# A block of unused TensorE products and cross-engine sums added inside the third FFN chunk

## The chip, the cores and the metric

The kernel runs on one core of one Trainium2 chip. The time is that of one execution on the device, in microseconds (us); lower is better. The core has a matrix engine (TensorE, "PE" in the profile, with "PEld" for its weight loads), a vector engine (VectorE, "DVE"), a scalar engine (ScalarE, "ACT"), GpSimd ("POOL") and SyncE ("SP"), which here only issues DMAs. Each engine runs its own instruction stream in order; the streams meet through semaphores.

## The reference

It is one transformer block with adaptive layer norm: linear attention, then a SwiGLU feed-forward network (FFN). S = 2048 rows, D = 1024, F = 3584, everything in bf16.

```python
sa, ca, ga, sb, cb, gb = (silu(c) @ w_mod) in six parts of 1024
h = layernorm(x) * (1 + ca) + sa
x = x + ga * linear_attention(h, wqkv, wo)       # 32 heads
h = layernorm(x) * (1 + cb) + sb
x = x + gb * ((silu(h @ w_gate) * (h @ w_up)) @ w_down)
```

## The kernel before

The program is written as plain Python calls, `P.pe(...)`, `P.act(...)`, `P.dve(...)`, `P.pool(...)` and `P.dma(...)`. A small planner, `_Prog`, notes for each call which bytes of SBUF and which PSUM banks it touches, and adds a semaphore wait wherever a call must come behind one of another engine. The order of the calls is the order of each engine's stream; nothing is rescheduled. For SBUF the planner knows reads from writes (a write waits for the last write and the last reads of the same bytes). For PSUM it does not: a bank belongs to the engine that used it last, and another engine that touches it waits. All compute instructions are recorded by one helper, so in the profile they all carry its line, L176 (L177 in the changed kernel).

The attention half takes the first part of the span. The FFN then goes over the 2048 rows in four chunks (`ch` 0 to 3) of 512 rows. The third chunk is `ch == 2`. A chunk has two stages:

- *Gate and up.* 28 steps (`ft` 0 to 27), one for each 128 columns of F. A step is eight 128x128x512 products of `GUG` with `H2T` into a gate bank and eight of `GUU` with `H2T` into an up bank. Then ACT takes Silu of the gate bank into `SG`, and DVE multiplies that with the up bank into `AT`. Even steps use banks 2 (gate) and 3 (up), odd steps banks 0 and 1. So the products of step `ft` have to wait until ACT and DVE have read what step `ft - 2` left in the same banks.
- *Down.* Four tiles of 128 rows (`j`), each 56 products of `AT` with `WD` (`WD_A` holds the first 16 blocks of w_down, `WD_B` the other 12) into a pair of banks, 4 and 5 or 6 and 7 by turns. ACT copies a bank out to `ATT`, DVE scales it and adds it to the residual `XRES`, and SP writes it out.

Weights for gate and up are loaded by SP into four slots, each as soon as TensorE has left it. During steps 4 to 7 of a chunk DVE also normalises the rows of the next one into `XN2`; after step 27 a DMA transposes them into `H2T` and POOL applies scale and shift (`th2_mod`).

The calls of a step, as they stand in the loop:

```python
P.act("activation", out=SG[:, ft % 2, :], in_=PS[:, gbank, :], func=ACT.Silu)
P.dve("tensor_tensor", out=AT[:, ft, :], in0=SG[:, ft % 2, :], in1=PS[:, ubank, :], op=ALU.mult)
```

Of the kernel before, what the change touches and what calls it, by code (L numbers as in the profile page):

```python
# [4 lines left out]

FP32 = mybir.dt.float32
BF16 = mybir.dt.bfloat16
U8 = mybir.dt.uint8
ACT = mybir.ActivationFunctionType
ALU = mybir.AluOpType  # L10
# [252 lines left out]
def bass_adaLN_cond__linear_attn_block__swiglu_ffn__prompt_kernel(  # L263
# [22 lines left out]
    with ExitStack() as es:  # L286
# [6 lines left out]
        def T(name, off, shape, dt):  # L293
            n = 1
            for s_ in shape[1:]:
                n *= s_
            assert off % 32 == 0 and off + n * mybir.dt.size(dt) <= ARENA, (name, off, shape)
            return nc.alloc_sbuf_tensor_at(name, shape, dt, offset=base + off)

        KB = 1024  # L300
        XRES = T("xres", 0, [128, NST, D], BF16)
        PQT = T("pqt", 32 * KB, [128, NHG, S], BF16)
        WCA = T("wca", 32 * KB, [128, NDT, D], BF16)
        WSA = T("wsa", 48 * KB, [128, NDT, D], BF16)
        AT = T("at", 72 * KB, [128, NFT, 512], BF16)
        SM = 64 * KB
        IDENT = T("ident", SM + 0, [128, 128], BF16)
        MASK = T("mask", SM + 256, [128, 128], BF16)
# [4 lines left out]
        MODTMP = T("modtmp", SM + 1088, [128, 16], BF16)  # L313
        MODCOL = T("modcol", SM + 1120, [128, 4, NDT], FP32)
        STATS = T("stats", SM + 1248, [128, 2, 4, 2, 6], FP32)
        MV = T("mv", SM + 1632, [128, NST, 2], FP32)
        VE = T("ve", SM + 1760, [128, NST], FP32)
        RSTD = T("rstd", SM + 1824, [128, NST], FP32)
        NEGHALF = T("neghalf", SM + 1888, [128, 4], FP32)
        SUMX = T("sumx", SM + 1920, [128, NST], FP32)  # L320
# [41 lines left out]
        WD_A = T("wd_a", 32 * KB, [128, 16, D], BF16)  # L362
# [7 lines left out]
        ATT = T("att", 190 * KB, [128, 2, 512], BF16)  # L370
        SG = T("sg", 184 * KB, [128, 2, 512], BF16)
        JUNK = T("junk", 186 * KB, [128, D], BF16)

        WDG = T("wdg", 144 * KB, [128, NFT, 128], BF16)

# [3 lines left out]
        PS = nc.alloc_psum_tensor("ps", [128, 8, 512], FP32)  # L379
# [15 lines left out]
        P = _Prog()  # L395
# [315 lines left out]
        def macc(src, kt):  # L711
            if kt == 0:
                P.dve("tensor_scalar", out=ACC[:], in0=src[:, kt, :], scalar1=SILUF[:, kt:kt + 1], scalar2=None,
                      op0=ALU.mult)
            else:
                P.dve("scalar_tensor_tensor", out=ACC[:], in0=src[:, kt, :], scalar=SILUF[:, kt:kt + 1], in1=ACC[:],
                      op0=ALU.mult, op1=ALU.add)

        def macc_split():
            P.dve("tensor_copy", out=MHL[:, 0, :], in_=ACC[:])  # L720
            P.dve("tensor_tensor", out=MHL[:, 1, :], in0=ACC[:], in1=MHL[:, 0, :], op=ALU.subtract)
            xbar(MHLT[:], MHL[:].rearrange("p i d -> p (i d)"))

        def mod_red():
            P.dve("tensor_reduce", out=RED[:], in_=MHLT[:].rearrange("d (i m) p -> d m i p", i=2),
                  axis=mybir.AxisListType.XY, op=ALU.add)
# [337 lines left out]
        def ln2_sq(st):  # L1064
            P.act("activation", out=JUNK[:], in_=XRES[:, st, :], func=ACT.Square, accum_out=SUMSQ[:, st:st + 1])
            if st % 4 == 3:
                ln2_rstd(st // 4)

        def gu_load(q):
            slot = q % 4  # L1070
            p = q % 14
            g_out, g_in = GUG[slot][:], wgv[:, :, p * 256:(p + 1) * 256]
            u_out, u_in = GUU[slot][:], wuv[:, :, p * 256:(p + 1) * 256]

            def fn(e):
                return [e.dma_start(out=g_out, in_=g_in), e.dma_start(out=u_out, in_=u_in)]

            P.add("sp", fn, reads=[], writes=[g_out, u_out], lane="gu%d" % slot, ninc=2, tag="gu_load")

        for st in range(NST):  # L1080
# [3 lines left out]
            if st < 4:  # L1084
                P.wait_for("sp", [done])
                if st < 3:
                    ch = st + 1
# [23 lines left out]
        for ch in range(NCH):  # L1111
            nxt = ch + 1 if ch + 1 < NCH else None
            for ft in range(NFT):
                q = 14 * ch + ft // 2
                slot = q % 4
                ftl = ft % 2
                gbank, ubank = 2 - (ft % 2) * 2, 3 - (ft % 2) * 2
                for dt in range(NDT):
                    P.pe("matmul", out=PS[:, gbank, :], lhsT=GUG[slot][:, dt, ftl * 128:(ftl + 1) * 128],
                         rhs=H2T[:, dt, :], start=(dt == 0), stop=(dt == NDT - 1))  # L1120
                for dt in range(NDT):
                    P.pe("matmul", out=PS[:, ubank, :], lhsT=GUU[slot][:, dt, ftl * 128:(ftl + 1) * 128],
                         rhs=H2T[:, dt, :], start=(dt == 0), stop=(dt == NDT - 1))
                P.act("activation", out=SG[:, ft % 2, :], in_=PS[:, gbank, :], func=ACT.Silu)
                P.dve("tensor_tensor", out=AT[:, ft, :], in0=SG[:, ft % 2, :], in1=PS[:, ubank, :], op=ALU.mult)
                if ftl == 1 and q + 4 < 14 * NCH:
                    gu_load(q + 4)
                if ch == 0 and ft % 2 == 0 and ft < 14:
                    i = ft // 2
                    wt = WD_A[:, 4 * i:4 * i + 4, :] if i < 4 else WD_B[:, 4 * i - 16:4 * i - 12, :]  # L1130
                    P.dma("wd%d" % i, wt, wdv[:, 4 * i:4 * i + 4, :])
                if ch == 0 and ft < 8:
                    macc(STGX[1], ft)
                if ch == 0 and ft == 8:
                    macc_split()
                if ch == 0 and ft == 11:
                    mod_red()
                    mod_row_a()
                if ch == 0 and ft == 12:
                    mod_row_b(6, 1, GB_B)  # L1140
                if nxt is None and ft in (8, 12):
                    f0, f1 = (0, 16) if ft == 8 else (16, NFT)
                    wt = WD_A if ft == 8 else WD_B
                    P.dve("tensor_tensor", out=WDG[:, f0:f1, :], in0=wt[:, :, 896:1024],
                          in1=GB_B[:, 896:1024].unsqueeze(1).to_broadcast([128, f1 - f0, 128]), op=ALU.mult)
                if nxt is not None and 4 <= ft < 8:
                    ln2_xn(4 * nxt + (ft - 4))
            if nxt is not None:
                th2_dma()
                th2_mod()  # L1150
            for j in range(4):
                st = 4 * ch + j
                bb = 4 + 2 * (st % 2)
                last = st == NST - 1
                if not last:
                    for ft in range(NFT):
                        for nh in range(2):
                            P.pe("matmul", out=PS[:, bb + nh, :], lhsT=AT[:, ft, j * 128:(j + 1) * 128],
                                 rhs=WD(ft)[:, nh * 512:nh * 512 + 512], start=(ft == 0), stop=(ft == NFT - 1))
                for nh in range(2):  # L1160
                    i = nh
                    parts = [(0, 384, bb + 1), (384, 512, 4)] if last and nh == 1 else [(0, 512, bb + nh)]
                    for (c0, c1, pb) in parts:
                        if last:
                            for ft in range(NFT):
                                P.pe("matmul", out=PS[:, pb, c0:c1], lhsT=AT[:, ft, j * 128:(j + 1) * 128],
                                     rhs=WDG[:, ft, :] if c0 > 0 else WD(ft)[:, nh * 512 + c0:nh * 512 + c1],
                                     start=(ft == 0), stop=(ft == NFT - 1))
                        xs = XRES[:, st, nh * 512 + c0:nh * 512 + c1]
                        gbs = GB_B[:, nh * 512 + c0:nh * 512 + c1]  # L1170
                        if c0 > 0:
                            P.dve("tensor_tensor", out=xs, in0=PS[:, pb, c0:c1], in1=xs, op=ALU.add)
                        else:
                            P.act("activation", out=ATT[:, i, c0:c1], in_=PS[:, pb, c0:c1], func=ACT.Copy)
                            P.dve("tensor_tensor", out=UT[:, i, c0:c1], in0=ATT[:, i, c0:c1], in1=gbs, op=ALU.mult)
                            P.dve("tensor_tensor", out=xs, in0=xs, in1=UT[:, i, c0:c1], op=ALU.add)
                        out_ops.append(P.dma("out", ov[:, st, nh * 512 + c0:nh * 512 + c1], xs))
# [37 lines left out]
```

## Time and profile before

| | |
|---|---|
| Measured times | 828.17 and 828.62 us, median 828.39 |
| Span of the profiled execution, first to last instruction | 827.0 us |
| TensorE busy | 817.0 us, 99% of the span, 4244 products recorded |
| VectorE busy | 310.8 us, 38% |
| ScalarE busy | 197.3 us, 24% |
| GpSimd busy | 40.7 us, 5% |
| Gate and up stage of the third chunk | from about 534.6 to 630.9 us of the span |

The profile is of one execution, of which the page gives the span; the measured times also contain what lies around it, 1.2 to 1.6 us here. In the lines of groups the columns are: kernel line, engine, operation, output <- inputs by tile name, shapes, count | busy time in us and mean duration of one in ns | idle time of the engine just before them, and what ended most of it. In the lines of the timeline they are: start and duration in us, engine, line, operation, tiles, shapes, count; in brackets the idle time before and what ended it. Products are pipelined: the duration of one includes the time until its result has drained, so the rate is read from starts, not from durations. Tile names are in lower case, `ps` is any PSUM bank.

### The profile page before, as it was taken

The numbers are of one execution on the slowest core, as the hardware profiler recorded it, in microseconds if no ns is written. First come the engines' busy times: TensorE is split into PE (matmuls) and PEld (weight loads), VectorE is DVE, ScalarE is ACT, GpSimd is POOL, SyncE is SP. The second block draws the span as 40 slices with busy tenths as digits, with TensorE's granted clock in tenths as the row PEclk, the third lists the DMA queues.
The fourth block names the chain that finished last, engine by engine and source line by source line (L and its number), as shares of the span: only waits on it lengthen the run. The fifth ranks groups of instructions, "written<-read, shape, count | busy, mean of one in ns | idle before, by whom it ended". The sixth has DMA issues, their size and how long they took to land.

```text
span 827.0 us, 10428 instructions
## 1 busy us (share of the span) xinstructions
PE 817.0 (99%) x4244; PEld 376.1 (45%) x4323; DVE 310.8 (38%) x664; ACT 197.3 (24%) x336; POOL 40.7 (5%) x59
## 2 busy tenths in 40 slices
PE   8999999999999999999999999999999999999998
PEld 4544444444444444444444444444444444444444
DVE  5798988476945521111221112122111211221111
ACT  4658643123241111011111101111110111111011
POOL 1010000000130000030000003000000300000000
PEclk9999999999999999999999999999999999999999
DMA  9969665856697995700455570045557004553000
GB/s 317 283 151 225 156 169 144 185 166 200 164 256 234 289 256 153 175 27 23 133 149 152 154 177 29 20 128 153 152 153 185 26 19 124 153 153 87 0 26 26
DMA packets 199360, 119.32 MB, mean 144 GB/s; under 512 B 57992, under 2 KB 183056, under 8 KB 199312
## 3 DMA queue, kind: packets, MB, share of 16 engines
q1 hardware_dynamic: 199296, 118.65, 53.7%
q8 instruction: 34, 0.56, 0.3%
q14 instruction: 14, 0.11, 0.0%
q10 hardware_dynamic: 16, 0.00, 0.0%
HBM read 100.67 MB, written 4.33 MB: 127 GB/s over the span
## 4 chain that ended last, share of the span: by engine, by line
PE 95%; DMA 2%; DVE 1%; SPq 1%; issue 1%; ACT 0%; DVEq 0%; ACTq 0%
PE ps L176 95%; DMA wsa<-in_w_mod_dram 2%; DVE acc L176 1%; SPq L176 1%; DVE pkt L176 0%; DVE e L176 0%; DVE pqt L176 0%; ACT e L176 0%; DVE xres L176 0%; DVE ht L176 0%; DVEq L247 0%; ACTq L247 0%
## 5 line engine op out<-in xcount | busy, mean ns | idle before, releaser
L176 PE MATMUL ps<-h2t,gug 128*128 128x512 bf16 x878 | 210.1, 379 | 0.9
L176 PE MATMUL ps<-h2t,guu 128*128 128x512 bf16 x878 | 209.9, 379 | 0.9
L176 DVE TENSOR_TENSOR at<-sg,ps 128x512 bf16<-128x512 bf16 x112 | 77.0, 688 | 282.7 <-PE ps L176 270.5
L176 ACT ACTIVATE sg<-ps 128x512 bf16<-128x512 f32 x112 | 66.9, 597 | 309.7 <-PE ps L176 298.3
L176 PEld LDWEIGHTS ps<-h2t,guu 128*128 128x128 bf16 x896 | 87.7, 98 | 105.7
L176 PEld LDWEIGHTS ps<-h2t,gug 128*128 128x128 bf16 x896 | 87.6, 98 | 105.5
L176 PE MATMUL ps<-wd_a,at 128*128 128x512 bf16 (+1 forms) x502 | 111.9, 377 | 0.5
L176 PE MATMUL ps<-ht,wqk 128*128 128x512 bf16 x499 | 110.5, 379 | 1.0 <-issue 0.2
L176 PE MATMUL ps<-wd_b,at 128*128 128x512 bf16 (+1 forms) x377 | 84.7, 377 | 0.4
L176 PEld LDWEIGHTS ps<-wd_a,at 128*128 128x128 bf16 x512 | 50.1, 98 | 59.7
L176 DVE TENSOR_TENSOR ut<-att,gb_b 128x512 bf16<-128x512 bf16 (+1 forms) x32 | 13.9, 435 | 167.2 <-ACT att L176 167.2
L176 PEld LDWEIGHTS ps<-ht,wqk 128*128 128x128 bf16 x512 | 49.4, 98 | 59.0 <-DVE ht L176 0.7
L176 ACT ACTIVATE att<-ps 128x512 bf16<-128x512 f32 (+1 forms) x32 | 17.4, 591 | 182.1 <-PE ps L176 182.1
L176 PEld LDWEIGHTS ps<-wd_b,at 128*128 128x128 bf16 x384 | 37.5, 98 | 44.7
L176 PE MATMUL ps<-pk,xres 128*128 128x512 bf16 x250 | 55.4, 379 | 0.6 <-issue 0.5
L176 PE MATMUL ps<-mw,pqt 128*128 128x512 bf16 x249 | 55.5, 379 | 0.5 <-issue 0.2
L176 POOL TENSOR_SCALAR h2t<-h2t,modcol 128x512 bf16<-128x512 bf16 x32 | 26.3, 837 | 383.4 <-DMA h2t<-xn 383.4
L176 ACT ACTIVATE e<-ps 128x512 bf16<-128x512 f32 x56 | 33.2, 604 | 31.9 <-PE ps L176 20.2
L176 PEld LDWEIGHTS ps<-mw,pqt 128*128 128x128 bf16 x256 | 24.7, 98 | 30.2 <-issue 0.5
L176 PEld LDWEIGHTS ps<-pk,xres 128*128 128x128 bf16 x256 | 24.7, 98 | 29.9 <-issue 0.9
L176 ACT ACTIVATE junk<-xres 128x1024 bf16<-128x1024 bf16 x24 | 25.4, 1058 | 34.5 <-DVE xres L176 34.2
L176 DVE SCALAR_TENSOR_TENSOR xres<-ps,xres 128x512 bf16<-128x512 f32 x32 | 21.4, 688 | 11.8 <-PE ps L176 11.6
(107 smaller groups left out, 337.9 us busy)
## 6 DMA issues: line engine op xcount, KB each, us to landing
gug<-in_B_w_gate_dram SPq DMA_DIRECT2D x56, 512.0 KB, 4.0
guu<-in_B_w_up_dram SPq DMA_DIRECT2D x56, 512.0 KB, 5.3
xres<-in_A_x_dram SPq DMA_DIRECT2D x20, 256.0 KB, 4.4
rb<-recip_den SPq DMA_DIRECT2D x8, 512.0 KB, 11.5
stgx<-in_w_mod_dram SPq DMA_DIRECT2D x2, 2048.0 KB, 9.7
wd_a<-in_B_w_down_dram SPq DMA_DIRECT2D x4, 1024.0 KB, 7.4
out_dram<-xres SPq DMA_DIRECT2D x31, 128.0 KB, 1.7
xres<-in_A_x_dram SPq DMA_DIRECT2D x3, 1024.0 KB, 7.1
```

The costliest lines, as they stand in the source:

```text
L176: return getattr(e, method)(**kw)
```

## The change

A function `probe()` is defined and called once, in the third chunk, behind the calls of step 16. Its results are used by nothing else. It has five new tiles, in SBUF bytes that are free during the FFN: `W4`, `X4` and `S4` in float32r, and three `F4` in float32. It reads `WD_A` (bf16), and uses PSUM banks 5 and 6.

```diff
+        W4 = T("w4", 100 * KB, [128, 4, 128], FP32R)
+        X4 = T("x4", 102 * KB, [128, 512], FP32R)
+        S4 = T("s4", 192 * KB, [128, 512], FP32R)
+        F4 = [T("f4%d" % i, (194 + 2 * i) * KB, [128, 512], FP32) for i in range(3)]
+
+        def probe():
+            b0, b1 = WD_A[:, 0, 0:512], WD_A[:, 1, 0:512]
+            P.dve("tensor_copy", out=W4[:].rearrange("p a b -> p (a b)"), in_=b0)
+            P.dve("tensor_copy", out=X4[:], in_=b1)
+            for i in range(32):
+                P.pe("matmul", out=PS[:, 5, :], lhsT=W4[:, i % 4, :], rhs=X4[:], start=(i == 0), stop=(i == 31))
+            for i in range(8):
+                P.pe("matmul", out=PS[:, 6, :], lhsT=W4[:, i % 4, :], rhs=X4[:], start=(i == 0), stop=False)
+                P.pe("matmul", out=PS[:, 6, :], lhsT=WD_A[:, i, 0:128], rhs=b0, start=False, stop=(i == 7))
+            for i in range(4):
+                P.act("activation", out=F4[0][:], in_=PS[:, 5, :], func=ACT.Copy)
+                P.dve("tensor_tensor", out=F4[1][:], in0=PS[:, 6, :], in1=F4[0][:], op=ALU.add)
+                P.pool("tensor_tensor", out=F4[2][:], in0=F4[1][:], in1=F4[0][:], op=ALU.add)
+                P.dve("tensor_tensor", out=F4[1][:], in0=F4[1][:], in1=F4[0][:], op=ALU.add)
+            for i in range(4):
+                P.dve("tensor_tensor", out=S4[:], in0=b0, in1=b1, op=ALU.subtract)
+                P.pool("tensor_tensor", out=S4[:], in0=b0, in1=b1, op=ALU.subtract)
+                P.act("activation", out=S4[:], in_=b1, func=ACT.Copy)
+                P.pool("tensor_copy", out=S4[:], in_=b1)
+            for i in range(4):
+                P.dve("tensor_tensor", out=S4[:], in0=b0, in1=F4[1][:], op=ALU.add)
+                P.pool("tensor_tensor", out=F4[2][:], in0=b0, in1=F4[0][:], op=ALU.add)
...
+                if ch == 2 and ft == 16:
+                    probe()
```

By the diff that is 48 products (40 float32r, 8 bf16), 18 instructions on DVE (two casts and 16 sums or differences), 16 on POOL (12 sums or differences, 4 copies) and 8 copies on ACT.

## The prediction

> **What bounds the kernel now.** I read the chain of waits first: it says which engine sets the end. Then the page's groups of instructions for durations, and last the timeline where the new work goes in.
>
> ```profile
> PE 95%; DMA 2%; DVE 1%; SPq 1%; issue 1%; ACT 0%; DVEq 0%; ACTq 0%
> ...
> L176 PE MATMUL ps<-h2t,gug 128*128 128x512 bf16 x878 | 210.1, 379 | 0.9
> L176 PE MATMUL ps<-h2t,guu 128*128 128x512 bf16 x878 | 209.9, 379 | 0.9
> L176 DVE TENSOR_TENSOR at<-sg,ps 128x512 bf16<-128x512 bf16 x112 | 77.0, 688 | 282.7 <-PE ps L176 270.5
> L176 ACT ACTIVATE sg<-ps 128x512 bf16<-128x512 f32 x112 | 66.9, 597 | 309.7 <-PE ps L176 298.3
> ```
>
> TensorE is 95% of the chain and idles 0.9 us before all 878 gate products, while DVE and ACT idle some 300 us waiting for it. So whatever TensorE is given is paid in full, and whatever the others are given is free until TensorE has to wait for it. The timeline at step 16 of the third chunk:
>
> ```profile
> 591.44 1.89 PE L176 MATMUL ps<-h2t,guu 128*128 128x512 bf16 x8
> 591.72 0.60 ACT L176 ACTIVATE sg<-ps 128x512 bf16<-128x512 f32 x1 [2.86 <-PE ps L176]
> ...
> 593.16 1.89 PE L176 MATMUL ps<-h2t,gug 128*128 128x512 bf16 x7
> 593.36 0.69 DVE L176 TENSOR_TENSOR at<-sg,ps 128x512 bf16<-128x512 bf16 x1 [2.76 <-PE ps L176]
> ```
>
> Step 16's up products start at 591.44 and step 17's gate products at 593.16: eight take 1.72 us, 0.2158 us each (the 379 ns of a row include the drain). A whole step is 16 products, 3.453 us. DVE's multiply starts 0.20 us after the next group has begun: that is how long a finished bank takes to be seen.
>
> **The change part by part.** Nothing is removed or moved. The instructions are inserted on PE, ACT, DVE and POOL between step 16 and step 17; no DMA is added, and SP is not touched.
>
> *1. The start.* The first float32r product waits for two DVE casts, which stand behind step 16's multiply on DVE. That multiply ends at 593.36 + 0.69 = 594.05. A cast of 512 elements between bf16 and f32 is a row: rcb<-rcp, 427 ns. Two give 594.91, a hop DVE to PE is 0.05 (mrow ends 289.05, the weight load begins 289.10). TensorE, free at 593.16, starts at 594.96: **1.8 us**, hidden by nothing.
>
> *2. The products.* 8 bf16 products at 0.2158 are 1.73. No row shows a float32r product. [...] Above: the weight load (98 ns in bf16) with twice the bytes and no longer beside the previous product, 0.2158 + 2 x 0.098 = 0.41. I take 0.2158, the row of the same shape: 40 x 0.2158 = 8.63. **10.4 us** together; the upper end adds 7.8.
>
> [...]
>
> *3. The chain behind the products.* The sums and copies share few buffers, so each waits for another engine. From bank 6's end, in the order of the waits in the compiled streams:
> - first loop, four turns: ACT copies bank 5 into f4[0], DVE adds bank 6, POOL adds the two, DVE adds again (it overwrites what POOL reads), and the next ACT copy overwrites f4[0], so it waits for both. The first ACT copy lies beside the last 16 products.
> - second loop, four turns: DVE, POOL, ACT, POOL, all writing s4, strictly one after the other.
> - third: four DVE sums behind the last POOL copy, with four POOL sums beside them.
>
> Prices: DVE sum with f32 0.69 (at<-sg,ps 688; den<-ps 683); ACT copy 0.60 (att<-ps 595). Hops: into POOL 0.12 (0.08 to 0.16 after DVE's ve), others 0.05. POOL has no 512-wide sum of two tensors. Nearest is its one-input row:
>
> ```profile
> L176 POOL TENSOR_SCALAR h2t<-h2t,modcol 128x512 bf16<-128x512 bf16 x32 | 26.3, 837 | 383.4 <-DMA h2t<-xn 383.4
> ```
>
> So a POOL sum lies between 0.84 and twice that, 1.67, if the inputs are read in turn; I take 1.2, nearer the one-input row. A POOL copy lies between 0.55 (a 256-wide memset at 0.311, scaled) and 0.84; I take 0.7. DVE's last four sums run beside POOL, which costs; see three lines of chunk 2's end, where POOL is busy from 641.16 to 647.91, and one later line without POOL:
>
> ```profile
> 644.48 0.88 DVE L176 TENSOR_TENSOR xres<-xres,ut 128x512 bf16<-128x512 bf16 x1
> 645.27 0.41 DVE L176 TENSOR_TENSOR ut<-att,gb_b 128x512 bf16<-128x512 bf16 x1
> 645.72 0.80 DVE L176 TENSOR_TENSOR xres<-xres,ut 128x512 bf16<-128x512 bf16 x1
> ...
> 656.48 0.42 DVE L176 TENSOR_TENSOR xres<-xres,ut 128x512 bf16<-128x512 bf16 x1
> ```
>
> Beside POOL the sum takes up to 0.4 more; I take 0.9 each (0.69 to 1.1).
>
> Loop one: 0.69 + 0.12 + 1.2 + 0.05 + 0.69 = 2.75, then three turns of 2.75 + 0.05 + 0.60 + 0.04 = 3.44: 13.1. Loop two: 0.69 + 0.12 + 1.2 + 0.05 + 0.60 + 0.12 + 0.7 + 0.05 = 3.53, four times 14.1. Loop three 3.6. Sum 30.8.
>
> *4. Who waits for it.* ACT and DVE run in order. Step 17's Silu is queued behind ACT's last probe copy, step 17's multiply behind DVE's last probe sum. Steps 17 and 18 still go, since banks 0 to 3 are two steps deep and steps 15 and 16 have been read. Step 19 reuses step 17's banks: its gate products wait for ACT, its up products for DVE. Cover after the last probe product: two steps and a gate, 6.91 + 1.73 = 8.63. Step 17's multiply ends 0.20 + 30.8 + 0.69 = 31.7 after it, plus a hop 31.75. TensorE loses 31.75 - 8.63 = **23.1 us**. Multiply and Silu of step 18 are queued right behind, and step 20 finds its banks free; from there the old rhythm holds. Weight loads on SP are triggered by TensorE's progress and land early; POOL's next task, the transposed chunk after step 27, comes more than 30 us later.
>
> *5. The clock.* TensorE starts slow after idling, though the granted clock reads 1.00 in those slices:
>
> ```profile
> 2.61 5.73 PE L176 MATMUL ps<-e,ident 128*128 128x512 bf16 x13 [0.24 <-DVE e L176]
> ...
> 9.10 1.24 PE L176 MATMUL ps<-e,ident 128*128 128x512 bf16 x5
> ```
>
> The first thirteen 512-wide products come 0.427 apart ((5.73 - 0.6) / 12), the later five 0.216 ((1.24 - 0.38) / 4). Here TensorE idles some 20 us from the end of step 18 (6.9 after the last probe product) until step 17's Silu (27.2). If the next thirteen run slow again, eight are step 19's gate products, from 27.2 to 30.6, still ahead of the multiply at 31.75, so their loss is covered; five more cost 5 x 0.211 = **1.05 us**. Ends: 0, and 2.7 with no cover.
>
> [...]
>
> **Sum:** 1.8 + 10.4 + 23.1 + 1.05 = 36.35 us. The rows come from an execution with a span of 827.0; the measured times, 828.17 and 828.62, stand 1.2 to 1.6 above it and that margin is untouched. 828.39 + 36.4 = **864.8 us**, 4.4% slower.
>
> **The rivals.**
> - *Slow float32r products* (0.22): more than one pass or loads in series. For: four bytes instead of two, no row. Against: only that the shape is the same. At 0.41 each the time is 864.8 + 7.8 = 872.6.
> - *Not slower by 2%* (0.02): the chain ends inside its cover. If it ended by 8.63 us, only the start and the products stay: 828.39 + 12.2 = 840.6, 1.5% more. It decides from there up to a chain of 13 us, where 2% is reached. Against: 36 operations in a row would have 0.36 us each, hops included, less than the 0.42 of the plain bf16 sums above.
> - *The waits are not as serial as I read them* (0.06): POOL's or ACT's part runs beside DVE's. DVE alone has 17 operations (8 + 4 + 4 sums and the multiply), 11.7 us without hops; with half of the other engines' time hidden the stall falls from 23.1 to about 13.5 and the time to 855.
>
> My forecast has 0.70. **Range:** downward, POOL at 0.84 and 0.55 (-2.9, -0.6), third-loop sums at 0.69 (-0.8), the four bf16 subtractions at 0.42 (-1.1), no slow clock (-1.05): 858.3. Upward, POOL at 1.67 and 0.84 (+3.8, +0.6), sums at 1.1 (+0.8), clock +1.7, float32r at 0.41 (+7.8): 879.5. So 858 to 880. About 2% is what a measurement of this kernel can tell from no change: slower 0.97, within 0.02, faster 0.01 (nothing is taken off TensorE).
>
> **What would show it.** In the profile after: 48 products on w4/x4 and wd_a at 0.216 apart after a gap of 1.8 us; one gap of some 20 us in TensorE after step 18, ended by ACT's sg, and a short one ended by DVE's at; then a few products 0.427 apart. I am wrong if the float32r products lie further apart, if POOL's sums are far from 1.2, or if step 19 does not wait.

## The result and the profile after

The changed kernel takes 868.25 us (867.88 and 868.63) against 828.39: a ratio of 1.0482, 95% interval 1.0451 to 1.0512. That is 39.9 us more, where 36.4 were forecast and 858 to 880 was the range. The profiled execution has a span of 865.9 us and a time of 867.88.

The chain of waits of the changed kernel, and its groups of gate and up products and of the new float32r products, as on the page and in the groups by form (the profile names float32r operands of products `f32`):

```profile
PE 95%; DVE 2%; POOL 1%; ACT 1%; issue 0%; DMA 0%; SPq 0%; DVEq 0%; POOLq 0%; ACTq 0%
...
L177 PE MATMUL ps<-h2t,gug 128*128 128x512 bf16 x896 | 213.1, 381 | 20.1 <-ACT sg L177 20.1
L177 PE MATMUL ps<-h2t,guu 128*128 128x512 bf16 x896 | 213.0, 381 | 3.8 <-DVE at L177 3.8
...
L177 PE MATMUL ps<-x,w 128*128 128x512 f32 x40 | 11.0, 425 | 1.5 <-DVE x L177 1.5
```

The last column shows where TensorE waits: it idles 20.1 us before gate products, waiting for ACT's Silu, 3.8 us before up products, waiting for DVE's multiply, and 1.5 us before the new products. On the chain DVE, which had 1% before, now has 2%, and POOL, which had none, has 1%. The timeline around step 16 to 20, without weight loads and SP:

```profile
590.60 1.89 PE L177 MATMUL ps<-h2t,guu 128*128 128x512 bf16 x8
590.88 0.60 ACT L177 ACTIVATE sg<-ps 128x512 bf16<-128x512 f32 x1 [2.86 <-PE ps L177]
...
593.13 0.42 DVE L177 CAST w<-wd_a 128x512 fp32r<-128x512 bf16 x1
593.47 0.42 DVE L177 CAST x<-wd_a 128x512 fp32r<-128x512 bf16 x1
...
593.95 7.78 PE L177 MATMUL ps<-x,w 128*128 128x512 f32 x33 [1.45 <-DVE x L177]
...
605.01 1.89 PE L177 MATMUL ps<-h2t,gug 128*128 128x512 bf16 x8
605.21 0.69 DVE L177 TENSOR_TENSOR f<-ps,f 128x512 f32<-128x512 f32 x1 [11.32 <-PE ps L177]
...
619.23 0.68 DVE L177 TENSOR_TENSOR s<-wd_a 128x512 fp32r<-128x512 bf16 x1
...
632.22 3.37 PE L177 MATMUL ps<-h2t,gug 128*128 128x512 bf16 x8 [20.14 <-ACT sg L177]
632.31 5.86 POOL L177 TENSOR_TENSOR f<-wd_a,f 128x512 f32<-128x512 bf16 x4
632.39 6.33 DVE L177 TENSOR_TENSOR s<-wd_a,f 128x512 fp32r<-128x512 bf16 x4 [2.60 <-POOL s L177]
...
638.64 1.27 DVE L177 TENSOR_TENSOR at<-sg,ps 128x512 bf16<-128x512 bf16 x2
639.37 3.21 PE L177 MATMUL ps<-h2t,guu 128*128 128x512 bf16 x8 [3.78 <-DVE at L177]
642.42 1.89 PE L177 MATMUL ps<-h2t,gug 128*128 128x512 bf16 x8
```

From this the bill is read off, each start against the one that the old rhythm would give. Eight products take 1.727 us there, so step 17's gate products would have started at 590.60 + 1.73 = 592.33, and the five groups of steps 17, 18 and 19's gate cover 8.63 us:

| term | read from | forecast | measured |
|---|---|---|---|
| start | 593.95 - 592.33 | 1.8 | 1.62 |
| 48 products | 605.01 - 593.95 | 10.4 | 11.06 |
| wait at step 19 | 639.37 - 605.01 - 8.63 | 23.1 | 25.73 |
| slow up products | 642.42 - 639.37 - 1.73 | 1.05 | 1.32 |
| sum | | 36.35 | 39.73 |

Spans alone give 865.9 - 827.0 = 38.9. The difference of 0.8 us lies before the change: in the kernel before, step 16's Silu starts at 591.72, here at 590.88. In the ten traces of this case that Silu starts anywhere from 590.88 to 592.83, although the kernels are alike up to it. The differences are there already at the first Silu of the FFN (246.88 to 248.82); from that one to step 16's all ten take 344.0. So below, beside the whole times, stands the **stretch** from step 16's Silu to the end of the span, which leaves that out: 827.0 - 591.72 = 235.28 before, 865.9 - 590.88 = 275.02 after, and 275.02 - 235.28 = 39.74, the sum of the table.

### The profile page after: what moved, and what is told of

The parts are those of the page before. It is cut to its first block, busy times and chain, and to the rows that moved or that the text cites. A ratio compares the mean times of both kernels' runs of the same rounds, so it can differ in the third digit from the quotient of the medians.

```text
span 865.9 us, 10657 instructions
## 1 busy us (share of the span) xinstructions
PE 835.2 (96%) x4371; PEld 384.4 (44%) x4371; DVE 326.1 (38%) x682; ACT 202.0 (23%) x344; POOL 58.3 (7%) x75
## 4 chain that ended last, share of the span: by engine, by line
PE 95%; DVE 2%; POOL 1%; ACT 1%; issue 0%; DMA 0%; SPq 0%; DVEq 0%; POOLq 0%; ACTq 0%
PE ps L177 95%; DVE s L177 1%; POOL s L177 1%; DVE f L177 1%; POOL f L177 1%; DMA xres<-in_A_x_dram 0%; ACT s L177 0%; ACT f L177 0%; DVE at L177 0%; DVE stats L177 0%; ACT xres L177 0%; SPq L177 0%; DVE x L177 0%; DVE w L177 0%; DVE xres L177 0%
## 5 line engine op out<-in xcount | busy, mean ns | idle before, releaser
L177 PE MATMUL ps<-h2t,gug 128*128 128x512 bf16 x896 | 213.1, 381 | 20.1 <-ACT sg L177 20.1
L177 PE MATMUL ps<-h2t,guu 128*128 128x512 bf16 x896 | 213.0, 381 | 3.8 <-DVE at L177 3.8
L177 POOL TENSOR_SCALAR h2t<-h2t,modcol 128x512 bf16<-128x512 bf16 x32 | 26.4, 842 | 287.7 <-DMA h2t<-xn 287.7
L177 POOL TENSOR_TENSOR rstd<-ve,neghalf 128x1 f32<-128x1 f32 (+2 forms) x17 | 12.9, 772 | 222.4 <-DVE ve L177 182.2
```

Source lines behind the costliest of these rows:

```text
L177: return getattr(e, method)(**kw)
```

## The experiments

The theory: TensorE pays for the products directly, and for the sums only because step 17's Silu and multiply are queued behind a chain in which each engine waits for another. Its rivals: the sums or products slow something by themselves (memory shared with TensorE, the form of the operation, the clock). Each ratio is against the kernel before, run on the same chip in the same rounds. That took 828.39 us for the change, 828.71 for products only, for the spread version and for the two of the third loop, and 828.59, on another chip, for the other four. Each kernel has one trace, so a stretch is that of one execution.

| run | time, us | ratio, 95% interval | stretch over before, us |
|---|---|---|---|
| the change | 868.25 | 1.0482 (1.0451-1.0512) | 39.74 |
| products only | 841.04 | 1.0149 (1.0134-1.0164) | 12.67 |
| chain only | 857.96 | 1.0351 (1.0333-1.0368) | 27.89 |
| all, spread over ten steps | 841.38 | 1.0153 (1.0138-1.0168) | 12.67 |
| third loop without POOL | 863.85 | 1.0426 (1.041-1.0441) | 35.00 |
| third loop, DVE from PSUM | 863.98 | 1.0425 (1.0407-1.0442) | 35.03 |
| gap of 3.8 us filled | 867.79 | 1.0468 (1.0452-1.0483) | 38.49 |
| second loop, split buffers | 861.85 | 1.0398 (1.0382-1.0413) | 33.09 |
| products in float32 | 866.08 | 1.0453 (1.0438-1.0469) | 37.84 |

The last column is the span minus the start of step 16's Silu in each trace, minus 235.28.

### Products only, and the chain only

```diff
 (products only)
-            for i in range(4):
-                P.act("activation", out=F4[0][:], ...)
...
 (chain only)
-            P.dve("tensor_copy", out=W4[:]..., in_=b0)
...
-                P.pe("matmul", out=PS[:, 6, :], lhsT=WD_A[:, i, 0:128], rhs=b0, ...)
```

> Leaves out every sum and copy behind the products; the two casts and the 48 products stay. Theory: start 1.6 and 48 products at 0.230, 11.1 together 12.7: 841.1, and no low clock. If the products themselves leave something behind (a lower clock, a slower rhythm of step 17 on): more than 842.

> Leaves out the two casts and the 48 products; all sums and copies stay (ACT and DVE read what the second chunk left in banks 5 and 6). TensorE goes straight from step 16 to 17, and DVE starts the chain behind step 16's multiply, 0.8 after TensorE is free. Theory: the chain up to step 17's multiply takes the 34.1 us that it took behind the products, the cover is the same 8.63, so TensorE loses 0.8 + 34.1 + 0.1 - 8.6 = 26.4, and between 0 and 1.7 for the second slow clock: 828.4 + 26.4 + 1.3 = 856.1. If products and chain share the loss in another way, for example if the slow sums come from TensorE's traffic: below 850.

They take 841.04 and 857.96 us. The products alone cost 12.67 in the stretch, the first two rows of the bill (1.62 + 11.06 = 12.68), and leave nothing behind: the granted clock is 1.00 and the next groups start 1.73 apart. The chain alone costs 27.89, read off its own trace, where step 17's gate products start at 594.27:

```profile
629.25 3.46 PE L177 MATMUL ps<-h2t,guu 128*128 128x512 bf16 x8 [3.56 <-DVE at L177]
...
632.54 1.89 PE L177 MATMUL ps<-h2t,gug 128*128 128x512 bf16 x8
```

The wait is 629.25 - 594.27 - 8.63 = 26.35 and the slow up products cost 632.54 - 629.25 - 1.73 = 1.56, together 27.91. In the stretch the two parts add up to 40.56, 0.82 more than the change. Of that 0.61 is the start of the chain: alone it begins 0.81 us after TensorE is free for step 17 (595.08 - 594.27), behind step 16's multiply, and in the change 0.20 after the last probe product. Another 0.24 is in the slow products (1.56 against 1.32). So the two parts explain the change to within 0.1 us. The whole time of the chain only stands 29.4 above before, 1.5 more than its stretch. In its trace the part ahead of the change is 1.1 us longer than in that of before (Silu at 592.83 against 591.72); why is not shown. So 857.96 lies 1.9 above the expectation, and the stretch 0.2 above what it had for the cost (27.89 for 26.4 + 1.3).

### The same work, spread over steps 17 to 26

```diff
+        def turn(k):            # k < 4: one turn of loop one, k < 8: of loop two,
...                              # then two turns of loop three
                 if ch == 2 and ft == 16:
                     probe()
+                if ch == 2 and 17 <= ft < 27:
+                    turn(ft - 17)
```

> All 90 instructions are kept, but the sums and copies are called one turn after each of the steps 17 to 26 instead of all behind step 16. If TensorE's loss is the queue (steps 17's Silu and multiply behind the whole chain): no gap at step 19, only the start, 1.6, and the products, 11.1, remain: 841.1. A turn on DVE is about 3.6 us against a step of 3.45, so a lag of under 1 us builds up, inside the cover of two steps. If the loss is the work itself (engines sharing memory with TensorE, or slow buffers): the time stays well above, 855 to 868.

It takes 841.38 us, and the stretch is 12.67 over before, the same as with no sums at all. All sums and copies are there, and cost nothing that the stretch shows. So the 27 us of the change are not the work of ACT, DVE and POOL; they are the place of that work in ACT's and DVE's queues. The timeline shows TensorE going on without a gap from step 26's up products to step 27's gate products, although DVE and POOL run the third loop's sums beside each other there, slow as in the change (two DVE sums in 2.72 us):

```profile
639.08 1.89 PE L177 MATMUL ps<-h2t,guu 128*128 128x512 bf16 x8
...
639.70 5.87 POOL L177 TENSOR_TENSOR f<-wd_a,f 128x512 f32<-128x512 bf16 x4
640.26 2.72 DVE L177 TENSOR_TENSOR s<-wd_a,f 128x512 fp32r<-128x512 bf16 x2
640.80 1.89 PE L177 MATMUL ps<-h2t,gug 128*128 128x512 bf16 x8
```

Of versions that keep the added work this is the cheapest that was run. Casting the operands two steps earlier should take off the start's 1.6 us as well; that has not been measured.

### What made DVE's last four sums slow

```diff
 (without POOL)
-                P.pool("tensor_tensor", out=F4[2][:], in0=b0, in1=F4[0][:], op=ALU.add)
 (from PSUM)
-                P.dve("tensor_tensor", out=S4[:], in0=b0, in1=F4[1][:], op=ALU.add)
+                P.dve("tensor_tensor", out=S4[:], in0=PS[:, 6, :], in1=F4[1][:], op=ALU.add)
```

> Leaves out the four POOL sums of the third loop. In the changed kernel DVE's four sums beside them took 1.56 us each instead of 0.69. If POOL beside them is the cause (theory): 0.69 each, step 17's multiply ends about 3.5 us earlier, step 19's up products start some 0.3 us behind its gate products, and the clock is not lowered a second time, which takes off another 1.3: 868.25 - 3.5 - 1.3 = 863.5. If the form of the sum itself is slow (bf16 and f32 in, float32r out): 1.56 each again and 868.2. If the clock needs as long to come back as at the start of the kernel, thirteen slow products: 864.8, with five slow up products.

> The third loop keeps all its sums, but DVE reads its first operand from PSUM bank 6 instead of SBUF. If what collides is DVE's second SBUF operand with POOL: 0.69 each on DVE and 863.5, as without POOL's sums. If any DVE sum beside POOL is slowed: 1.56 each and 868. In between: one SBUF operand collides less than two.

They take 863.85 and 863.98 us, both near the 863.5 of the theory. The groups by form of these sums in the changed kernel:

```profile
L177 DVE TENSOR_TENSOR s<-wd_a,f 128x512 fp32r<-128x512 bf16 x4 | 6.2, 1556 | 2.7 <-POOL s L177 2.6
...
L177 POOL TENSOR_TENSOR f<-wd_a,f 128x512 f32<-128x512 bf16 x4 | 5.6, 1405 | 0.2
```

without POOL's sums:

```profile
L177 DVE TENSOR_TENSOR s<-wd_a,f 128x512 fp32r<-128x512 bf16 x4 | 2.8, 692 | 2.7 <-POOL s L177 2.6
```

and with DVE's first operand from PSUM:

```profile
L177 DVE TENSOR_TENSOR s<-ps,f 128x512 fp32r<-128x512 f32 x4 | 2.8, 692 | 2.7 <-POOL s L177 2.6
...
L177 POOL TENSOR_TENSOR f<-wd_a,f 128x512 f32<-128x512 bf16 x4 | 4.7, 1163 | 0.2
```

The form is not slow: alone it takes 692 ns. POOL beside it is not enough either: with one operand in PSUM the two run side by side at 692 and 1163 ns. With two SBUF operands on DVE, beside POOL sums that read two as well, a DVE sum takes 1556 ns and a POOL sum 1405. The single records of the trace show what the price follows: in the change each of the four DVE sums ends 0.55 us after the POOL sum beside it (634.02 and 633.47 for the first), as if it had waited for that one's end. That DVE's second SBUF operand is what collides rests on these three runs; the mechanism behind it they do not show. The price is that a DVE sum takes 2.25 times as long (1556 against 692 ns).

### Filling the second gap

```diff
                 (step 19, between its gate and its up products)
+                if ch == 2 and ft == 19:
+                    for i in range(12):
+                        P.pe("matmul", out=PS[:, 7, :], lhsT=WD_A[:, i, 0:128], rhs=WD_A[:, 0, 0:512], ...)
```

> All of the change, and 12 bf16 products more in bank 7 between step 19's gate and up products, where TensorE stands idle for 3.8 us waiting for DVE. They take 2.6 us once the clock is up. Theory: the idle time there lowers the clock a second time, so with it filled step 19's up products run at 0.216 instead of 0.427 and the time falls by 1.3, to 866.9, although products were added. If the clock stays low for as long as at the start, whatever is between: 868.2, up products slow. If the added products delay something: 869 to 871.

It takes 867.79 us. The whole time is 0.5 below the change's, too little to be told from it with confidence; the changed kernel was not in the same rounds. The stretch shows the expected 1.25 less (38.49 against 39.74), although 12 products were added, and the timeline shows why:

```profile
633.38 3.60 PE L177 MATMUL ps<-h2t,gug 128*128 128x512 bf16 x8 [20.15 <-ACT sg L177]
...
636.76 3.88 PE L177 MATMUL ps<-wd_a 128*128 128x512 bf16 x12
...
640.53 1.90 PE L177 MATMUL ps<-h2t,guu 128*128 128x512 bf16 x8
642.27 1.89 PE L177 MATMUL ps<-h2t,gug 128*128 128x512 bf16 x8
```

Step 19's up products take 1.74 instead of 3.05. What was not expected: the clock did not come up during step 19's gate products, as it did in the change, but only with the filling (granted 0.50 in every stretch of one microsecond from 633 to 639, then 0.99; in the change 0.88 already from 635 to 636). The first six fillers ran slow too, 0.43 us apart by their weight loads. That is taken up in the last section. Filling both gaps, which might keep the clock up throughout, has not been measured.

### Buffers of their own in the second loop

```diff
-                P.pool("tensor_tensor", out=S4[:], in0=b0, in1=b1, op=ALU.subtract)
-                P.act("activation", out=S4[:], in_=b1, func=ACT.Copy)
-                P.pool("tensor_copy", out=S4[:], in_=b1)
+                P.pool("tensor_tensor", out=S4P[:], in0=b0, in1=b1, op=ALU.subtract)
+                P.act("activation", out=S4A[:], in_=b1, func=ACT.Copy)
+                P.pool("tensor_copy", out=S4P[:], in_=b1)
```

> All of the change, but in the second loop POOL and ACT write tiles of their own instead of the s4 that DVE writes. If it is the shared output that makes the loop serial (theory): DVE's eight sums of loops two and three run on end beside POOL's twelve operations, at 0.69 to 1.56 each, 5.5 to 12.5 instead of 19.4 us: 854 to 861. If the engines would have been as slow without it (their work is the bound): 866 to 868.

It takes 861.85 us, 0.9 above the upper end of the expectation. The shared output does make the loop serial: without it ACT's four copies run back to back and DVE no longer waits. But only 6.65 us of the stretch go (39.74 to 33.09), because the collision and the clock take part of the wait's place:

```profile
619.27 1.55 DVE L177 TENSOR_TENSOR f<-f,f 128x512 f32<-128x512 f32 x1 [1.54 <-POOL f L177]
...
620.75 5.22 DVE L177 TENSOR_TENSOR s<-wd_a 128x512 fp32r<-128x512 bf16 x4
...
626.00 5.11 DVE L177 TENSOR_TENSOR s<-wd_a,f 128x512 fp32r<-128x512 bf16 x4
...
631.77 3.60 PE L177 MATMUL ps<-h2t,guu 128*128 128x512 bf16 x8 [8.20 <-DVE at L177]
635.16 3.13 PE L177 MATMUL ps<-h2t,gug 128*128 128x512 bf16 x8
```

Beside POOL, DVE's nine sums take some 1.3 us each instead of 0.69: from 619.27 to 631.04, 11.8 us where 6.2 would do. In loops two and three the single records go by turns: a DVE sum takes 1.0 to 1.1 us beside a POOL copy (0.95 there, 0.61 alone) and 1.52 beside a POOL sum, and each again ends 0.55 us after the POOL instruction beside it. TensorE's gap before the up products grows to 8.2 us, and the clock is low for all of them and most of the next gate products (granted 0.50 in the stretches of one microsecond from 628 to 637, 0.67 in the next). Slow products cost 1.66 + 1.24 = 2.9 us here, 1.6 more than in the change. The expectation had counted DVE's sums, not that. The split together with DVE reading from PSUM, which should take the collision away too, has not been measured.

### Plain float32 products

```diff
 (products only, and)
-        W4 = T("w4", 100 * KB, [128, 4, 128], FP32R)
-        X4 = T("x4", 102 * KB, [128, 512], FP32R)
+        W4 = T("w4", 100 * KB, [128, 4, 128], FP32)
+        X4 = T("x4", 102 * KB, [128, 512], FP32)
```

> Products only, with the 40 float32r products in plain float32; every sum and copy behind them is left out. If float32 takes four passes: 40 x 0.863 + 8 x 0.216 = 36.3, and 1.6 for the start: 866.3. If float32 runs at the rate of float32r: 841.0, as with the products alone. Two passes at half the rate or so: 850.

It takes 866.08 us, by four times the bf16 price for each float32 product; but they do not appear as four. The groups by form:

```profile
L177 PE MATMUL ps<-x,w 128*128 128x512 f32 x80 | 35.7, 593 | 1.5 <-DVE x L177 1.5
```

40 products appear as 80, and the weight loads in the timeline are 0.43 us apart with the granted clock at 1.00: two records of half the rate for each product, 0.86 us. Whether a record is two passes the trace does not say. The same tiles declared float32r appear as 40 products at 0.23. So plain float32 has the first of the three prices in the expectation, 0.86 a product for the 0.863 there, and float32r does not.

## Why the prediction was right, point by point

**What bounds** held: every microsecond of the 39.74 is TensorE's: added work, waiting or slow products. The sums cost nothing where TensorE does not wait for them (spread).

**1. The start** was 1.62 for 1.8. The second cast starts at 593.47 while the first, from 593.13, takes 0.42: the casts start 0.34 apart, not 0.43, and the first starts 0.09 before the row of the multiply in front of it ends (592.53 + 0.69 = 593.22).

**2. The products** were 11.06 for 10.36: the mis-sized term is the float32r rate, 0.230 ((7.78 - 0.43) / 32) instead of 0.2158. The eight pairs of float32r and bf16 come 0.46 apart, so the two together cost two times 0.230; how they share it is not shown, nor why 0.230. By the prediction's own sign of being wrong the products do lie further apart, by 0.014 us each, and that cost 0.7. The rival of slow float32r products (0.41) fell.

**3. The chain**, 31.75 forecast from the last probe product to step 19's up products, took 34.36. Loop one took 14.0 (605.21 to 619.23) for 13.1, with POOL's sum at 1.26 for 1.2 and hops of about 0.1 instead of 0.05. Loop two took 13.2 (619.23 to 632.39) for 14.1, with POOL's sum at 1.15 and its copy at 0.61 for 0.7. These two errors cancel: step 19's gate products start 27.21 after the last probe product (632.22 - 605.01), where 27.2 was forecast, and so close a hit is luck. The lower bound of the copy, 0.55, is not what its row gives either: 0.311 doubled is 0.62, and with the step from the 128-wide memset (0.204) it is 0.53.

Loop three is the term that was mis-sized: 6.25 (632.39 to 638.64) for 3.6. The prediction read from chunk 2's end that a DVE sum beside POOL takes up to 0.4 more. In those rows it went from 0.42 to 0.88, which is 0.46 more and 2.1 times as long, and the single records show what that follows: both sums end 0.27 us after the POOL instruction beside them (645.08 and 645.35, 646.25 and 646.52). So what POOL costs there does not carry over as a fixed amount: it depends on the POOL instruction. Beside POOL's sums, which take 1.16 where DVE reads from PSUM and not 0.77 as the scaling instructions before DVE began there, a DVE sum takes 1.56. Whether the number of operands that POOL reads matters besides, no run separates.

**4. Who waits** was right to the step: gate products of step 19 wait for ACT, up products for DVE, steps 17 and 18 run free, and the rhythm is back at step 20.

**5. The clock** came to 1.32 for 1.05, but the mechanism that was forecast, thirteen slow products from one start, is not what happened, so that the sizes lie close is luck. The clock was back 3 us after the gate products began; the wait for DVE, 3.8 us instead of the 1.15 forecast, took it down a second time. Mean granted clock in five stretches of one microsecond of the changed kernel (the columns are the stretch, its length, busy time and count of PE, PEld, DVE, ACT and POOL, the granted clock, the DMA share and GB/s):

```profile
614.00:615.00 1.00, 0.00 (x0) 0.00 (x0) 0.11 (x1) 0.00 (x0) 0.79 (x1) 0.88 0.00 0
...
635.00:636.00 1.00, 0.60 (x2) 0.00 (x0) 0.97 (x2) 0.00 (x0) 0.92 (x2) 0.88 0.00 0
...
638.00:639.00 1.00, 0.00 (x0) 0.00 (x0) 1.00 (x2) 0.00 (x0) 0.17 (x1) 0.83 0.00 0
639.00:640.00 1.00, 0.63 (x2) 0.28 (x3) 0.91 (x2) 0.60 (x1) 0.00 (x0) 0.50 0.00 0
...
642.00:643.00 1.00, 1.00 (x6) 0.45 (x5) 0.38 (x1) 0.00 (x0) 0.00 (x0) 0.97 0.00 0
```

So the collision of DVE and POOL was paid twice: 3.5 us of longer sums, and 1.3 for the clock that the longer gap let fall. Both are gone together when either POOL's sums or DVE's second SBUF operand is taken away (4.74 and 4.71 us of the stretch). In the change the gate group alone did bring the clock back, 3.0 us after it began (632.22 to 635.24), where thirteen products at 0.427 would have taken 5.55. It is not so in every run, since with the gap filled the same start stayed slow for 5.6 us (633.38 to 639.02).

**The rivals.** The chain did not end inside its cover, and the waits are as serial as they were read; what became of them without the shared buffer is shown by the split.

## What to carry to other kernels

Whether work for mostly idle engines is free depends on where it stands in their queues. Put one turn behind each step, within the lead that TensorE's double buffers give, it cost nothing here (a stretch 12.67 us over before with the sums and without); put in one block, the same work cost 27 us. When pricing a chain, ask of each pair of operations that run side by side on DVE and POOL how many operands DVE reads from SBUF (here, beside POOL's sums, 1556 ns a sum with two and 692 with one) and how long POOL's instruction takes (here a DVE sum ended 0.55 us after a POOL sum, 0.27 after a scaling). And ask of each gap in TensorE's work whether it is long enough to lower the clock, as the 3.8 us before step 19's up products were here: the slow products, 1.32 us there, then come on top of the gap.

## What the runs showed of the hardware that was not expected

**In these traces the clock changes on a grid of 3.41 us.** Within a stretch of one microsecond whose mean lies between 0.50 and 1.00, the moment of the change can be worked out. In the changed kernel that gives a fall at 614.76, a rise at 635.24, a fall at 638.66 and a rise at 642.06: distances of 20.48, 3.42 and 3.40, that is 6, 1 and 1 times 3.41 us. The other traces that were read this way agree (gap filled: fall 618.54, rise 639.02, 20.48 apart; split buffers: 617.18, 624.00, 627.42 and 637.66, which is 2, 1 and 3 times 3.41). The author's estimate from these distances and the shares that follow is that the clock is decided once every 3.41 us by how busy TensorE was in the window just past; no run was made to test it. Windows with TensorE at work for 79% (639.37 to 642.06 in the change) and 88% (632.22 to 635.24 there) of their length raised it; windows with 65% (gap filled, from 633.38 to 635.61) and 73% (split buffers, from 631.77 to 634.25) did not. Windows with 10% (635.24 to 635.59 in the change) and 21% (611.35 to 612.08 there) lowered it, one with about 44% (gap filled, 611.72 to 613.22) did not. Where between these shares the limits lie, and whether the share is all that counts, is not shown. Such a grid would explain why the same slow start lasted 3.0 us in one run and 5.6 in another: it would depend on where in the window the work begins.

**The granted clock at the kernel's start** reads 1.00 while products come 0.427 apart, in all of these traces as in the one before. The traces hold no record of the clock for that stretch: the first one is a rise at 8.31 us in the kernel before, at 7.19 in the changed kernel and at 6.19 with split buffers, and of the first thirteen products all thirteen, ten and nine come 0.43 apart. So the column says nothing there, and thirteen was no fixed number: from 7.19 to the fall at 614.76 are 607.57 us, 178 windows of 3.413 us. Later in the span the column agrees with the distances: in the changed kernel weight loads come 0.43 apart at 0.50 (632.62 to 634.76), and groups of eight products start 1.73 apart at 1.00, 0.216 each (605.01 to 610.19).

**Plain float32** appears as two products at half the rate, 0.86 us together, float32r as one at 0.230 us, 7% above bf16.
